# Loading the weights of an attention and gated-MLP kernel in pieces on SyncE's queue, with smaller first tiles and warm products

## The chip, the cores and the metric

The kernel runs on one core of one Trainium2 chip. The metric is the device time of one execution in microseconds (us). Runs come in a fast and a slow state (e9 below: 256.56 to 257.29 us and 263.62 to 265.26 us); only fast runs are compared. "Faster" or "slower" needs 2%.

The engines are named as in the profile: PE is TensorE (PEld its weight load), DVE VectorE, ACT ScalarE, POOL GpSimd, SP SyncE. In the traces TensorE took its products in the order in which the program lists them (compared up to the first `psp` product: 342 products in the changed kernel, 303 in the one before). The weight loads issued on GpSimd convert float32 to float16 on the way (the page of the kernel before counts 256 KB for each of the eight of w_in, whose float32 source is 512 KB); those issued on SyncE bring the float32 bytes (16 of 256 KB for the same matrix), which engines then cast.

## The reference

For each of 8 batches the kernel computes grouped attention (16 query heads, 4 key heads, 384 positions, 64 numbers a head), puts the heads side by side to rows of 1024, and sends them through a gated MLP:

```python
attn = softmax(q @ k.T / 8) @ v            # 16 heads, k and v shared by 4
h = np.maximum(x @ w_in, 0.0)              # w_in 1024 x 1024
u, v = h[..., :512], h[..., 512:]
v_n = (v - mean) / sqrt(var + 1e-6)
v_s = einsum('ts,bsd->btd', w_spatial, v_n) + b_spatial
out = (u * v_s) @ w_out                    # w_out 512 x 1024
```

Inputs and outputs are float32; the products use float16. In this text the "V products" are those with the second half of w_in, the "U group" those with the first half, and "po" those with w_out.

## The kernel before

The program is a written list of steps. Each step goes to the end of the queue of each engine that it uses, so the list fixes the order in which each engine is given its instructions. `lwi` and `lwo` load weights, `lk lq lv` load inputs, `ck cq cv` cast them, `S` is a score product, `E` its exp, `X` the product with v, `V` and `G,..,gu` the V and U products.

```python
FIRST = """                                   # cut to a few steps
lk,0,0,2 lq,0,0,0,1,s cq,0,0,0,1,0,v ck,0,0,s Tk,0,0 cq,0,0,0,1,1,s lk,0,2,4 Tq,0,0,0 ...
lwi,0,1,3 cq,0,0,1,3,0,p lwi,0,1,0 ... lwi,0,1,2 lwi,0,1,1 ... V,0,0,0,4 V,0,0,4,8 ...
... lwi,0,0,2 ... lwi,0,0,0 lwo,0,1 ... lwi,0,0,3 lwi,0,0,1 ... lwo,0,0 ...
"""

    def load_w_in(part, g):                   # one of 8; converts while it loads
        c0, c1 = part * DH, (part + 1) * DH
        nc.gpsimd.dma_start(
            w_in16[32 * g : 32 * (g + 1), :, c0:c1],
            moe_w_in[g * G * D : (g + 1) * G * D, c0:c1].rearrange("(kc r) n -> r kc n", r=32),
        )

    def v_mm(b, st, k0=0, k1=NKT):            # V products: need w_in16[:, kc, 512:1024]
        ...
        for kc in range(k0, k1):
            nc.tensor.matmul(
                held["pv", b, st],
                xT[b][:, kc, st * P : (st + 1) * P],
                w_in16[:, kc, DH:DFF],
                start=(kc == 0), stop=(kc == NKT - 1),
            )
```

Chunk `kc` of `w_in16` needs four groups of 32 rows of w_in that lie 256 rows apart: partition 32g+r holds row 256g+32kc+r.

The softmax here doesn't subtract the row's maximum and nothing guards it: scores larger than these inputs give would overflow.

## Time and profile before

The median of the first three runs is 257.8 us (257.32 to 258.01). The one profile at hand was of a run of 260.65 us, marked slow.

| what | before |
|---|---|
| TensorE busy from 50 to 240 us | 189.4 of 190 us |
| TensorE busy in the first 50 us | 38.4 us |
| wait of the first V products for w_in | 4.21 us |
| first U group | 53.12 us |
| span | 258.8 us |

From the profile page of the kernel before: busy time of TensorE with its share of the span, then busy tenths in 40 slices of 6.5 us.

```profile
PE 242.5 (94%) x2505; PEld 124.1 (48%) x2505; DVE 152.1 (59%) x287; ACT 182.8 (71%) x229; POOL 45.3 (18%) x92
...
PE   2985899899999999999999999999999999999993
...
DMA  7999999894994008995394909293582011300606
```

After the eighth slice TensorE is full. Up to it the DMA row is nearly always at 9: loads set the pace of the start.

The busy time by stretch, kernel before. The first pair is the stretch, the next number its length, then each engine's busy time, the granted clock of TensorE, the mean busy share of the DMA engines (overlapping packets can take it past 1) and GB/s.

```profile
25.00:30.00 5.00, 3.10 (x8) 1.02 (x8) 0.67 (x2) 0.42 (x1) 2.20 (x5) 0.58 1.06 334
0.00:50.00 50.00, 38.39 (x323) 15.87 (x325) 27.65 (x48) 34.65 (x42) 19.56 (x38) 0.93 1.06 219
50.00:240.00 190.00, 189.38 (x2104) 100.25 (x2099) 116.65 (x226) 144.08 (x181) 25.78 (x54) 1.00 0.55 145
```

From the timeline of TensorE, kernel before: start, length, instructions, and in brackets the idle time ahead of them and what ended it.

```profile
26.91 3.57 PE L441 MATMUL pv<-w_in,xt 128*128 128x512 f16 x8 [4.21 <-DMA w_in<-in_moe_w_in_dram]
...
53.12 0.82 PE L616 MATMUL pu<-xt,w_in 64*128 64x384 f16 x8
```

From the chain of waits of the kernel before, in order of time: start, length, what.

```profile
15.68 0.51 POOL w_in L241
16.19 10.58 DMA w_in<-in_moe_w_in_dram
```

One load of 256 KB took 10.58 us, while the DMA engines were full with it and others (busy share 1.06 from 25 to 30 us), and the first V products waited for it.

### The profile page before, as it was taken

Reading aid. Unit: us, or ns where it says so; the run is one execution under the profiler, and the core shown is the slowest. Engines: PE = TensorE matmul, PEld = TensorE weight load, DVE = VectorE, ACT = ScalarE, POOL = GpSimd, SP = SyncE. Lnnn points to the kernel's source line nnn. Section 1 sums busy time; section 2 is a strip of 40 time slices with the busy share of each in tenths; the row PEclk is TensorE's granted clock in tenths of the full one; section 3 lists DMA queues with packets and bytes.
Section 4 is the critical chain, followed back from the end, with each engine's and each line's share of the span. In section 5 each row is a group of like instructions: output and inputs, shape, how many; then the busy total and the mean of one; then the engine's idle time right before and its main releaser. Section 6 shows DMA issues by size and latency. Waiting matters only on the chain.

```text
span 258.8 us, 5938 instructions
## 1 busy us (share of the span) xinstructions
PE 242.5 (94%) x2505; PEld 124.1 (48%) x2505; DVE 152.1 (59%) x287; ACT 182.8 (71%) x229; POOL 45.3 (18%) x92
## 2 busy tenths in 40 slices
PE   2985899899999999999999999999999999999993
...
DMA  7999999894994008995394909293582011300606
GB/s 183 230 265 247 292 196 195 153 286 125 237 262 102 4 3 304 165 345 174 113 205 131 313 8 233 95 323 114 104 214 84 3 55 61 127 6 0 243 0 243
DMA packets 57578, 41.66 MB, mean 161 GB/s; under 512 B 26832, under 2 KB 53840, under 8 KB 57552
## 3 DMA queue, kind: packets, MB, share of 16 engines
...
## 4 chain that ended last, share of the span: by engine, by line
PE 83%; DMA 9%; DVE 4%; ACT 1%; POOL 0%; issue 0%; SPq 0%; ACTq 0%
PE X L398 18%; PE po L643 14%; PE pu L616 12%; PE sc L378 11%; PE pv L603 11%; PE pv L441 5%; DMA w_in<-in_moe_w_in_dram 4%; PE po L548 4%; PE pu L513 4%; PE psp L629 3%; DMA k<-in_k_dram 3%; DMA q<-in_q_dram 2%; DVE v_s L499 1%; DVE v_n L473 1%; PE psp L487 1%; ACT aT L389 1%
## 5 line engine op out<-in xcount | busy, mean ns | idle before, releaser
L389 ACT ACTIVATE aT<-sc 128x1024 f16<-128x1024 f32 x144 | 140.8, 1023 | 35.7 <-PE sc L378 35.3
L643 PE MATMUL po<-w_out,gT 64*128 64x512 f16 x288 | 68.0, 376 | 0.0
L603 PE MATMUL pv<-w_in,xt 64*128 64x512 f16 x272 | 64.9, 376 | 0.0
L378 PE MATMUL sc<-qT,kT 64*128 64x512 f16 x288 | 56.4, 396 | 1.4 <-DVE qT L308 0.5
L427 DVE TENSOR_TENSOR xt<-X,rec 128x512 f16<-128x512 f32 x48 | 31.2, 686 | 13.4 <-ACT rec L415 4.8
L308 DVE COPY osb<-po 128x512 f32<-128x512 f32 x39 | 26.6, 686 | 17.8 <-PE po L643 15.3
L616 PE MATMUL pu<-xt,w_in 64*128 64x384 f16 x384 | 36.7, 323 | 0.0
L398 PE MATMUL X<-aT,v 128*32 128x512 f16 x576 | 35.9, 379 | 0.0
L643 PEld LDWEIGHTS <-gT 64*128 64x128 f16 x288 | 25.4, 94 | 14.5 <-DVE mark_v L697 3.0
L603 PEld LDWEIGHTS <-xt 64*128 64x128 f16 x272 | 24.8, 94 | 12.5 <-issue 3.8
L308 POOL CAST q<-q 128x768 f16<-128x768 f32 (+2 forms) x34 | 24.4, 747 | 35.8 <-DMA q<-in_q_dram 33.2
L525 DVE SCALAR_TENSOR_TENSOR gT<-pu,v_s 128x384 f16<-128x384 f32 x31 | 16.1, 553 | 24.6 <-PE pu L616 20.9
L378 PEld LDWEIGHTS <-kT 64*128 64x128 f16 x288 | 17.1, 94 | 25.2 <-issue 16.9
L616 PEld LDWEIGHTS <-w_in 64*128 64x128 f16 x384 | 20.0, 94 | 13.3 <-issue 0.8
L499 DVE TENSOR_TENSOR v_s<-psp,bias_b 128x384 f32<-128x384 f32 x32 | 20.0, 688 | 5.6 <-PE psp L487 3.4
L398 PEld LDWEIGHTS <-v 128*32 128x32 f16 x576 | 15.9, 96 | 15.5 <-issue 1.6
L398 PE MATMUL X<-aT,ones 128*32 128x512 f16 x288 | 20.6, 392 | 0.5 <-DVE v_s L499 0.2
L409 ACT ACTIVATE rec<-X 128x512 f32<-128x512 f32 x22 | 13.1, 598 | 11.1 <-PE X L398 11.1
L462 DVE BATCH_NORM_STATS2 stats<-v_r 128x6 f32<-128x512 f32 x24 | 16.5, 686 | 5.6 <-ACT v_r L454 2.9
L699 POOL MEMSET mark_p<- 1x1 f32 x20 | 1.8, 88 | 101.4 <-PE psp L629 57.7
L441 PE MATMUL pv<-w_in,xt 128*128 128x512 f16 x56 | 15.3, 419 | 4.2 <-DMA w_in<-in_moe_w_in_dram 4.2
L629 PE MATMUL psp<-wsT,v_n 64*128 64x384 f16 x144 | 15.5, 323 | 0.9 <-DVE v_n L473 0.8
...
## 6 DMA issues: line engine op xcount, KB each, us to landing
...
```

Of the source, the lines that this page charges most:

```text
L308: engine.tensor_copy(dst, src)
L378: mm = nc.tensor.matmul(sc[:, half, :], kT[b][lo:hi, gp, t, :], rhs[lo:hi, :], start=True, stop=True)
L389: nc.scalar.activation(aT[b, qt][:, gp, t], held["sc", b, u], AF.Exp, scale=scale)
L398: nc.tensor.matmul(dst[32 * g : 32 * (g + 1), :], v16[:, g, t, 32 * part : 32 * (part + 1)] if part < 2 else ones32, a[:, g // 2, t, g % 2 ...
L427: nc.vector.tensor_tensor(xt[:, jj, :, qt * P : (qt + 1) * P], held["X", b, qt, jj].rearrange("p (j q) -> p j q", j=G), held["rec", b, qt] ...
L441: nc.tensor.matmul(held["pv", b, st], xT[b][:, kc, st * P : (st + 1) * P], w_in16[:, kc, DH:DFF], start=(kc == 0), stop=(kc == NKT - 1),)
L462: nc.vector.bn_stats(s6, held["v_r", b, st])
L499: nc.vector.tensor_tensor(held["v_s", b][:, m, :].rearrange("p (t s) -> p t s", t=NST), held["psp", b, m][:, 0:S].rearrange("p (t s) -> p ...
L603: yield lambda kc=kc: nc.tensor.matmul(held["pv", b, st], xT[b][rows, kc, st * P : (st + 1) * P], w_in16[rows, kc, DH:DFF], start=(first a ...
L616: yield lambda kc=kc: nc.tensor.matmul(held["pu", b, mu][:, 0:S], w_in16[rows, kc, mu * P : (mu + 1) * P], xT[b][rows, kc, :], start=(firs ...
L629: yield lambda st=st: nc.tensor.matmul(held["psp", b, m][:, 0:S], held["v_n", b, st][rows, m * P : (m + 1) * P], wsT16[rows, st, :], start ...
L643: yield lambda m=m: nc.tensor.matmul(held["po", b, i], held["gT", b][rows, m, tt * P : (tt + 1) * P], w_out16[rows, m, half * 512 : (half ...
```

## The change

The intent is to free GpSimd of its casting loads (8.6 us from issue to landing at the median for those of w_in), to let each V or U product start on a piece of weights instead of a quarter of all rows, and to start the first scores sooner:

1. All weights come as 24 float32 pieces of 256 KB on SyncE, into five staging buffers. GpSimd (16), VectorE (6) and ScalarE (2) cast them.
2. The first k tile comes alone, the first q tile in even and odd heads, each with a score product of half size.
3. 37 warm products of the identity fill TensorE's idle time near the start, in the hope of a higher clock at the scores.

The diff, cut to its core:

```diff
-    def load_w_in(part, g):
-        ...nc.gpsimd.dma_start(w_in16[32 * g : 32 * (g + 1), :, c0:c1], ...)
+    def load_w(part, i):
+        piece = stage.tile([P, 512], FP32, name=f"w32_{part}_{i}", tag="w32", bufs=5)
+        if part < 2:
+            src = moe_w_in.rearrange("(g kc r) n -> kc g r n", g=HKV, kc=NKT)[
+                i, :, :, part * DH : (part + 1) * DH
+            ]
+        else:
+            m, half = i // 2, i % 2
+            src = moe_w_out[m * P : (m + 1) * P, half * 512 : (half + 1) * 512]
+        nc.sync.dma_start(piece, src)
+        loaded["w32", part, i] = piece
+
+    def cast_w(part, i, engine):
+        ...copy(dst, loaded["w32", part, i], engine)
 ...
-    def score_mm(b, u):
+    def score_mm(b, u, j0=0, js=1):           # js=2: every second head, half the columns
 ...
+    def warm(b, n):
+        ...
+        for _ in range(n):
+            nc.tensor.matmul(dst, ident16, ident16, start=True, stop=True)
 ...
 FIRST (a few of its steps)
-lk,0,0,2 lq,0,0,0,1,s cq,0,0,0,1,0,v ck,0,0,s Tk,0,0 ...
+lq,0,0,1,3 lq,0,0,0,1,0,2,s W,0,3 cq,0,0,0,1,1,0,2,p ... lk,0,0,2,0,1 W,0,3 W,0,28 ...
+... lw,0,1,2 lq,0,1,1,3 lw,0,1,1 ... lw,0,1,0 lv,0 ... lw,0,1,3 ... lq,1,0 lk,1 lw,0,1,6 ...
+... lk,2 ... lq,2,1 ... lw,0,2,1 lw,0,2,2 lw,0,0,6 ... cw,0,0,6,p ... cw,0,0,3,s ...
```

`lw,0,1,2` loads piece 2 of the V half, `lw,0,0,6` piece 6 of the U half, `lw,0,2,..` pieces of w_out; `cw` casts a piece on GpSimd (p), VectorE (v) or ScalarE (s). The source of a w_in piece has the shape [4, 32, 512]: four row groups, 32 rows, 512 numbers.

More of the change, by code (lines that the diff above doesn't have):

```diff
@@ L16 @@
 DVE, ACT = mybir.EngineType.DVE, mybir.EngineType.Activation
+SPLIT = 1
 FIRST = """
-lk,0,0,2 lq,0,0,0,1,s cq,0,0,0,1,0,v ck,0,0,s Tk,0,0 cq,0,0,0,1,1,s lk,0,2,4 Tq,0,0,0 lq,0,1,0,1
-lq,0,0,1,3 lq,0,1,1,3 cq,0,1,0,1,1,p tq,0,0,0,v tk,0,0,s S,0 cq,0,1,0,1,0,v ck,0,1,v E,0 S,0
-lwi,0,1,3 cq,0,0,1,3,0,p lwi,0,1,0 cq,0,1,1,3,0,p Tk,0,1 lk,1 lv,0 Tq,0,1,0 tk,0,1,v tq,0,1,0,v S,0
-lq,1,0 cq,0,0,1,3,1,v E,0 E,0 lq,1,1 S,0 Tq,0,0,1 S,0 S,0 Tq,0,0,2 cq,0,1,1,3,1,p tq,0,0,1,v
-Tq,0,1,1 tq,0,1,1,v S,0 ck,1,1,p tq,0,0,2,v E,0 lwi,0,1,2 lwi,0,1,1 ck,1,0,p S,0 E,0 cv,0,p E,0
@@ L25 @@
-X,0,0,2 S,0 lv,1 lws,0 Tq,0,1,2 S,0 S,0 lbi,0 Tkk,1 rv,0,0 E,0 lk,2 S,0 X,0,0,0 X,0,0,1 lq,2,0
-lq,2,1 E,0 cq,1,0,0,1,1,p E,0 E,0 E,0 S,0 cq,1,0,1,3,0,p cq,1,0,1,3,1,p cq,1,0,0,1,0,p tq,0,1,2,v
-tkk,1,v cq,1,1,0,1,0,p S,0 E,0 xm,0,0,1 X,0,1,2 xm,0,0,0 X,0,1,0 X,0,1,1 S,0 S,0 V,0,0,0,4 V,0,0,4,8
-rv,0,1 S,0 S,0 E,0 E,0 E,0 E,0 cq,1,1,0,1,1,s xm,0,1,0 xm,0,1,1 Tqq,1,0 tqq,1,0,0,v V,0,1,0,4
-ru,0,0,v cq,1,1,1,3,0,v tqq,1,0,1,v cv,1,v E,0 E,0 S,0 S,0 E,0 X,0,2,0 X,0,2,2 X,0,2,1 lwi,0,0,2
-cws,0,0 cws,0,2 cq,1,1,1,3,1,p cws,0,1 lwi,0,0,0 lwo,0,1 cq,2,0,0,3,0,p lwi,0,0,3 lwi,0,0,1
@@ L31 @@
-cq,2,0,0,3,1,p cq,2,1,0,3,0,p ck,2,1,p lwo,0,0 ck,2,0,p cq,2,1,0,3,1,p E,0 rl,0,2 S,0 re,0,2 E,0 S,0
-xm,0,2,1 Tqq,1,1 E,0 xm,0,2,0 V,0,1,4,8 Tw,0,0,2 Tw,0,2,3 S,0 S,0 tqq,1,1,0,s ru,0,1,v tw,0,0,2
-V,0,2,0,4 V,0,2,4,8 bs,0,0 bs,0,1 ru,0,2,v tqq,1,1,1,v E,0 tw,0,2,3 bs,0,2 S,0 E,0 E,0 S,0 X,1,0,2
-rl,1,0 X,1,0,0 X,1,0,1 Tqq,1,2 S,0 re,1,0 S,0 xm,1,0,0 xm,1,0,1 V,1,0,0,4 E,0 dq,2,0 dk,2 V,1,0,4,8
-S,0 rs,0 tqq,1,2,0,v nm,0,2 E,0 tqq,1,2,1,v nm,0,0 nm,0,1 ru,1,0,v G,0,gs,0,0,0,1 S,0 G,0,gs,2,0,0,1
@@ L36 @@
-dq,2,1 lq,3,1 lk,3 E,0 mk,0,gs,0,v G,0,gs,0,1,0,1 S,0 lv,2 lq,3,0 mk,0,gs,2,v G,0,gs,2,1,0,1 E,0 E,0
-sa,0,0 sa,0,1 sa,0,2 sa,0,3 S,0 cq,3,1,0,3,1,p cq,3,1,0,3,0,p X,1,1,2 cq,3,0,0,3,0,p cq,3,0,0,3,1,p
-X,1,1,1 X,1,1,0 E,0 rl,1,1 re,1,1 ck,3,0,p xm,1,1,0 xm,1,1,1 G,0,gu,0,0,0 S,0 G,0,gu,0,0,1 E,0 S,0
-mk,0,gu,0,v G,0,gu,2,0,0 S,0 E,0 E,0 G,0,gu,0,1,0 S,0 G,0,gu,2,0,1 S,0 G,0,gu,0,1,1 mk,0,gu,2,v E,0
-E,0 E,0 bs,1,0 G,0,gu,2,1,0 S,0 G,0,gu,2,1,1 S,0 gt,0,0 E,0 X,1,2,0 gt,0,2 gt,0,3 gt,0,1 X,1,2,2
@@ L41 @@
-cv,2,v E,0 S,0 S,0 V,1,1,0,4 rl,1,2 V,1,1,4,8 S,0 G,0,go,0,0,0 G,0,go,0,0,1 mk,0,go,0,v S,0 re,1,2
-E,0 E,0 G,0,go,0,1,0 E,0 G,0,go,0,1,1 S,0 E,0 xm,1,2,0 oc,0,1,v oc,0,0,v E,0 X,2,0,2 X,1,2,1 rl,2,0
-xm,1,2,1 re,2,0 ru,1,1,s X,2,0,0 X,2,0,1 S,0 S,0 xm,2,0,0 G,1,w12,2,0,0 G,1,w12,2,0,1 S,0 S,0
-ck,3,1,s E,0 E,0 mk,1,w12,2,v xm,2,0,1 G,1,w12,2,1,0 bs,1,1 G,1,w12,2,1,1 oc,0,2,v ru,1,2,v oc,0,3,v
-E,0 bs,1,2 E,0 X,2,1,2 rl,2,1 re,2,1 X,2,1,0 dq,3,0 S,0 xm,2,1,0 G,2,w24,0,0,0 E,0 lq,4,0
-G,2,w24,0,0,1 S,0 lv,3 dk,3 lq,4,1 rs,1 st,0,0 mk,2,w24,0,p nm,1,0 dq,3,1 nm,1,1 X,2,1,1 S,0
@@ L47 @@
-G,2,w24,0,1,0 E,0 S,0 xm,2,1,1 E,0 oc,0,4,v G,2,w24,0,1,1 nm,1,2 E,0 G,1,gs,0,0,0,1 S,0 cv,3,p
-mk,1,gs,0,p ru,2,0,s oc,0,5,v S,0 G,1,gs,2,0,0,1 mk,1,gs,2,v E,0 G,1,gs,0,1,0,1 G,1,gs,2,1,0,1 S,0
-E,0 S,0 sa,1,0 sa,1,2 sa,1,1 E,0 E,0 sa,1,3 G,1,gu,0,0,0 G,1,gu,0,0,1 S,0 E,0 mk,1,gu,0,p
-G,1,gu,2,0,0 S,0 G,1,gu,2,0,1 S,0 G,1,gu,0,1,0 S,0 E,0 mk,1,gu,2,p G,1,gu,2,1,0 S,0 G,1,gu,0,1,1 E,0
-gt,1,1 gt,1,0 S,0 G,1,gu,2,1,1 E,0 X,2,2,2 E,0 rl,2,2 E,0 gt,1,3 gt,1,2 X,2,2,1 S,0 G,2,w10,1,0,0
-G,2,w10,1,0,1 S,0 E,0 S,0 re,2,2 E,0 mk,2,w10,1,v xm,2,2,1 bs,2,0 G,2,w10,1,1,0 G,2,w10,1,1,1
@@ L53 @@
-oc,1,0,v oc,1,1,v ru,2,1,v X,2,2,0 xm,2,2,0 bs,2,1 lv,4 st,1,0 lk,4 st,0,1 st,0,2 E,0
+lq,0,0,1,3 lq,0,0,0,1,0,2,s W,0,3 cq,0,0,0,1,1,0,2,p cq,0,0,0,1,0,0,2,v lk,0,0,2,0,1 W,0,3 W,0,28
+lq,0,0,0,1,1,2 lk,0,0,2,1,3 lk,0,2,4 lq,0,1,0,1 ck,0,0,0,1,v lw,0,1,2 lq,0,1,1,3 lw,0,1,1
+cq,0,0,0,1,0,1,2,s ck,0,0,1,3,s cq,0,0,1,3,1,0,1,p lw,0,1,0 lv,0 Tq,0,0,0,0,2 lw,0,1,3
+cq,0,0,0,1,1,1,2,p Tk,0,0,0,1 lq,1,0 lk,1 lw,0,1,6 cq,0,1,0,1,1,0,1,p lw,0,1,5 lw,0,1,4 Tq,0,0,0,1,2
+tk,0,0,0,1,v tq,0,0,0,0,2,v S,0 tq,0,0,0,1,2,v ck,0,1,0,3,v Tk,0,0,1,3 S,0 tk,0,0,1,3,v Tk,0,1,0,3
@@ new lines @@
+lw,0,1,7 S,0 S,0 E,0 E,0 cq,0,0,1,3,0,0,1,s cq,0,1,0,1,0,0,1,v tk,0,1,0,3,v Tq,0,1,0,0,1
+tq,0,1,0,0,1,v Tq,0,0,1,0,1 S,0 E,0 Tq,0,0,2,0,1 S,0 W,0,3 tq,0,0,1,0,1,v tq,0,0,2,0,1,v
+cq,0,1,1,3,0,0,1,v cq,0,1,1,3,1,0,1,v S,0 E,0 E,0 E,0 E,0 S,0 Tq,0,1,1,0,1 S,0 Tq,0,1,2,0,1 lq,1,1
+cv,0,p lws,0 tq,0,1,1,0,1,v cw,0,1,0,v cw,0,1,2,p cw,0,1,1,p cw,0,1,3,p tq,0,1,2,0,1,v lw,0,0,2 S,0
+E,0 cq,1,0,1,3,0,0,1,p cq,1,0,0,1,0,0,1,p cq,1,0,0,1,1,0,1,p ck,1,0,0,3,p lv,1 cw,0,1,5,p cw,0,1,7,p
+cq,1,0,1,3,1,0,1,p ck,1,1,0,3,p X,0,0,2 S,0 lw,0,0,3 X,0,0,1 lw,0,0,4 lw,0,0,0 rv,0,0 lq,2,0
@@ new lines @@
+cq,1,1,0,1,0,0,1,p E,0 E,0 E,0 lw,0,0,7 lw,0,0,5 lw,0,0,1 S,0 S,0 cws,0,0 X,0,0,0 E,0 S,0
+cq,1,1,1,3,0,0,1,p lbi,0 lk,2 E,0 X,0,1,2 E,0 rl,0,1 X,0,1,1 S,0 S,0 lq,2,1 E,0 lw,0,2,1 lw,0,2,2
+lw,0,0,6 E,0 cws,0,1 re,0,1 cw,0,0,2,p cws,0,2 cq,1,1,1,3,1,0,1,p xm,0,0,0 xm,0,0,1 cw,0,0,0,p
+Tk,1,0,0,3 tk,1,0,0,3,v cw,0,1,4,v cw,0,1,6,v V,0,0,0,4 X,0,1,0 cq,2,0,0,3,1,0,1,p S,0 Tq,1,0,0,0,1
+V,0,0,4,8 E,0 S,0 xm,0,1,0 xm,0,1,1 tq,1,0,0,0,1,v cw,0,0,4,p cw,0,0,5,p S,0 E,0 V,0,1,0,4
+Tk,1,1,0,3 E,0 S,0 X,0,2,2 cq,1,1,0,1,1,0,1,v ru,0,0,v E,0 Tq,1,1,0,0,1 V,0,1,4,8 rl,0,2
@@ new lines @@
+tq,1,1,0,0,1,s S,0 ru,0,1,v tk,1,1,0,3,v ck,2,1,0,3,p cq,2,0,0,3,0,0,1,p S,0 X,0,2,0 re,0,2 X,0,2,1
+cw,0,0,7,p cq,2,1,0,3,1,0,1,p E,0 S,0 cq,2,1,0,3,0,0,1,p xm,0,2,0 E,0 cw,0,2,1,p cw,0,0,6,p Tw,0,2,3
+Tq,1,0,1,0,1 E,0 cw,0,0,3,s xm,0,2,1 cv,1,v bs,0,0 V,0,2,0,4 S,0 tq,1,0,1,0,1,v tw,0,2,3 S,0
+Tq,1,1,1,0,1 V,0,2,4,8 tq,1,1,1,0,1,v bs,0,1 ru,0,2,v bs,0,2 E,0 S,0 E,0 X,1,0,2 S,0 E,0
+Tq,1,1,2,0,1 Tw,0,0,2 rl,1,0 tw,0,0,2 X,1,0,0 X,1,0,1 re,1,0 E,0 xm,1,0,0 rs,0 xm,1,0,1 S,0 S,0
+Tq,1,0,2,0,1 E,0 E,0 cw,0,0,1,s V,1,0,0,4 V,1,0,4,8 nm,0,0 S,0 nm,0,2 tq,1,1,2,0,1,v nm,0,1
@@ new lines @@
+tq,1,0,2,0,1,v G,0,gs,0,0,0,1 S,0 ru,1,0,v G,0,gs,2,0,0,1 mk,0,gs,0,v mk,0,gs,2,v ck,2,0,0,3,v
+dq,2,0 G,0,gs,0,1,0,1 E,0 dk,2 lw,0,2,0 lw,0,2,3 dq,2,1 G,0,gs,2,1,0,1 S,0 sa,0,1 sa,0,3 lw,0,2,5
+sa,0,0 sa,0,2 lw,0,2,7 lw,0,2,6 cw,0,2,3,p cw,0,2,5,p lw,0,2,4 cw,0,2,6,p cw,0,2,7,p E,0 E,0 S,0
+X,1,1,2 rl,1,1 re,1,1 X,1,1,1 X,1,1,0 lv,2 S,0 G,0,gu,0,0,0 lk,3 lq,3,1 lq,3,0 G,0,gu,0,0,1 E,0
+xm,1,1,0 cv,2,p xm,1,1,1 S,0 cw,0,2,2,v mk,0,gu,0,v cw,0,2,0,v G,0,gu,2,0,0 S,0 G,0,gu,2,0,1 S,0 E,0
+E,0 mk,0,gu,2,v G,0,gu,0,1,0 S,0 G,0,gu,0,1,1 S,0 G,0,gu,2,1,0 E,0 gt,0,0 gt,0,1 S,0 E,0 E,0 E,0 E,0
@@ new lines @@
+X,1,2,2 G,0,gu,2,1,1 S,0 gt,0,2 gt,0,3 cq,3,1,0,3,1,0,1,p ck,3,0,0,3,p cq,3,0,0,3,0,0,1,p
+ck,3,1,0,3,p cq,3,1,0,3,0,0,1,p cq,3,0,0,3,1,0,1,p S,0 V,1,1,0,4 E,0 rl,1,2 E,0 cw,0,2,4,v V,1,1,4,8
+S,0 E,0 G,0,go,0,0,0 S,0 G,0,go,0,0,1 mk,0,go,0,v ru,1,1,v S,0 G,0,go,0,1,0 G,0,go,0,1,1 oc,0,0,v
+oc,0,1,v S,0 E,0 E,0 re,1,2 X,2,0,2 X,1,2,0 rl,2,0 E,0 re,2,0 X,1,2,1 X,2,0,1 X,2,0,0 xm,1,2,0
+xm,1,2,1 xm,2,0,1 S,0 G,1,w12,2,0,0 G,1,w12,2,0,1 bs,1,0 xm,2,0,0 mk,1,w12,2,v S,0 S,0 E,0 E,0 E,0
+G,1,w12,2,1,0 G,1,w12,2,1,1 bs,1,1 oc,0,2,s ru,1,2,v X,2,1,2 X,2,1,0 X,2,1,1 S,0 S,0 bs,1,2 oc,0,3,v
@@ new lines @@
+rl,2,1 st,0,0 dq,3,0 dk,3 re,2,1 st,0,1 dq,3,1 xm,2,1,0 rs,1 E,0 lv,3 lq,4,0 G,2,w24,0,0,0
+G,2,w24,0,0,1 nm,1,0 mk,2,w24,0,v xm,2,1,1 nm,1,1 nm,1,2 S,0 S,0 G,2,w24,0,1,0 E,0 E,0 oc,0,4,v E,0
+G,2,w24,0,1,1 ru,2,0,s oc,0,5,v S,0 S,0 G,1,gs,0,0,0,1 G,1,gs,2,0,0,1 E,0 E,0 mk,1,gs,0,v
+mk,1,gs,2,v G,1,gs,0,1,0,1 G,1,gs,2,1,0,1 S,0 sa,1,0 sa,1,1 S,0 sa,1,3 sa,1,2 G,1,gu,0,0,0
+G,1,gu,0,0,1 G,1,gu,2,0,0 S,0 E,0 E,0 mk,1,gu,0,v bs,2,0 S,0 G,1,gu,0,1,0 E,0 E,0 G,1,gu,0,1,1 S,0
+G,1,gu,2,0,1 E,0 S,0 gt,1,1 gt,1,0 mk,1,gu,2,v X,2,2,1 X,2,2,2 S,0 G,1,gu,2,1,0 S,0 G,1,gu,2,1,1 E,0
@@ L54 @@
+rl,2,2 X,2,2,0 re,2,2 S,0 E,0 xm,2,2,1 gt,1,3 E,0 gt,1,2 G,2,w10,1,0,0 G,2,w10,1,0,1 mk,2,w10,1,v
+S,0 S,0 G,2,w10,1,1,0 xm,2,2,0 E,0 E,0 G,2,w10,1,1,1 E,0 ru,2,1,s lv,4 lq,4,1 lk,4 oc,1,0,v bs,2,1
+oc,1,1,v st,1,0 cv,3,p st,0,2
 """
 STEADY = """
-X,0,0,2 rl,0,0 re,0,0 X,0,0,0 X,0,0,1 S,0 E,0 xm,0,0,0 xm,0,0,1 ck,1,0,p ck,1,1,p cq,1,0,0,3,0,p
-cq,1,0,0,3,1,p cq,1,1,0,3,0,p cq,1,1,0,3,1,p cv,1,p dk,1 dq,1,0 dq,1,1 G,-1,w12,2,0,0 G,-1,w12,2,0,1
-mk,-1,w12,2,v S,0 E,0 S,0 E,0 G,-1,w12,2,1,0 oc,-2,2,v G,-1,w12,2,1,1 ru,-1,2,v oc,-2,3,v st,-2,1
@@ L60 @@
-bs,-1,2 X,0,1,2 rl,0,1 re,0,1 X,0,1,0 X,0,1,1 rs,-1 S,0 E,0 xm,0,1,0 xm,0,1,1 nm,-1,0 nm,-1,1
-G,0,w24,0,0,0 G,0,w24,0,0,1 mk,0,w24,0,v nm,-1,2 S,0 E,0 S,0 E,0 G,0,w24,0,1,0 oc,-2,4,v
-G,0,w24,0,1,1 ru,0,0,s oc,-2,5,v st,-2,2 bs,0,0 lk,2 lq,2,0 lq,2,1 lv,2 S,0 E,0 G,-1,gs,0,0,0,1
-mk,-1,gs,0,p S,0 E,0 G,-1,gs,2,0,0,1 mk,-1,gs,2,p G,-1,gs,0,1,0,1 sa,-1,0 sa,-1,1 S,0 E,0
-G,-1,gs,2,1,0,1 sa,-1,2 sa,-1,3 X,0,2,2 rl,0,2 re,0,2 X,0,2,0 X,0,2,1 S,0 E,0 xm,0,2,0 xm,0,2,1
-G,-1,gu,0,0,0 G,-1,gu,0,0,1 mk,-1,gu,0,p S,0 E,0 G,-1,gu,2,0,0 G,-1,gu,2,0,1 mk,-1,gu,2,p S,0 E,0
@@ L66 @@
-G,-1,gu,0,1,0 G,-1,gu,0,1,1 gt,-1,0 gt,-1,1 S,0 E,0 G,-1,gu,2,1,0 G,-1,gu,2,1,1 gt,-1,2 gt,-1,3 S,0
-E,0 S,0 E,0 G,0,w10,1,0,0 G,0,w10,1,0,1 mk,0,w10,1,v S,0 E,0 S,0 E,0 G,0,w10,1,1,0 oc,-1,0,v
-G,0,w10,1,1,1 ru,0,1,v oc,-1,1,v st,-1,0 bs,0,1 S,0 E,0
+X,0,0,2 rl,0,0 re,0,0 X,0,0,0 X,0,0,1 S,0 E,0 xm,0,0,0 xm,0,0,1 ck,1,0,0,3,p ck,1,1,0,3,p
+cq,1,0,0,3,0,0,1,p cq,1,0,0,3,1,0,1,p cq,1,1,0,3,0,0,1,p cq,1,1,0,3,1,0,1,p cv,1,p dk,1 dq,1,0
+dq,1,1 G,-1,w12,2,0,0 G,-1,w12,2,0,1 mk,-1,w12,2,v S,0 E,0 S,0 E,0 G,-1,w12,2,1,0 oc,-2,2,v
@@ new lines @@
+G,-1,w12,2,1,1 ru,-1,2,v oc,-2,3,v st,-2,1 bs,-1,2 X,0,1,2 rl,0,1 re,0,1 X,0,1,0 X,0,1,1 rs,-1 S,0
+E,0 xm,0,1,0 xm,0,1,1 nm,-1,0 nm,-1,1 G,0,w24,0,0,0 G,0,w24,0,0,1 mk,0,w24,0,v nm,-1,2 S,0 E,0 S,0
+E,0 G,0,w24,0,1,0 oc,-2,4,v G,0,w24,0,1,1 ru,0,0,s oc,-2,5,v st,-2,2 bs,0,0 lk,2 lq,2,0 lq,2,1 lv,2
+S,0 E,0 G,-1,gs,0,0,0,1 mk,-1,gs,0,p S,0 E,0 G,-1,gs,2,0,0,1 mk,-1,gs,2,p G,-1,gs,0,1,0,1 sa,-1,0
+sa,-1,1 S,0 E,0 G,-1,gs,2,1,0,1 sa,-1,2 sa,-1,3 X,0,2,2 rl,0,2 re,0,2 X,0,2,0 X,0,2,1 S,0 E,0
+xm,0,2,0 xm,0,2,1 G,-1,gu,0,0,0 G,-1,gu,0,0,1 mk,-1,gu,0,p S,0 E,0 G,-1,gu,2,0,0 G,-1,gu,2,0,1
@@ L69 @@
+mk,-1,gu,2,p S,0 E,0 G,-1,gu,0,1,0 G,-1,gu,0,1,1 gt,-1,0 gt,-1,1 S,0 E,0 G,-1,gu,2,1,0 G,-1,gu,2,1,1
+gt,-1,2 gt,-1,3 S,0 E,0 S,0 E,0 G,0,w10,1,0,0 G,0,w10,1,0,1 mk,0,w10,1,v S,0 E,0 S,0 E,0
+G,0,w10,1,1,0 oc,-1,0,v G,0,w10,1,1,1 ru,0,1,v oc,-1,1,v st,-1,0 bs,0,1 S,0 E,0
 """
@@ L204, in load_v, with load_q @@
         loaded["v32", b] = v32
-    def load_q(b, gp, t0=0, t1=NST, queue=None):
+    def load_q(b, gp, t0=0, t1=NST, j0=0, js=1, queue=None):
         if ("q32", b, gp) not in loaded:
@@ L210, in load_q @@
         (queue or nc.sync).dma_start(
-            loaded["q32", b, gp][:, :, t0 * D : t1 * D],
-            q[b, h0 : h0 + 2 * G].rearrange("h (p t) d -> p h (t d)", t=NST)[
+            loaded["q32", b, gp][:, j0::js, t0 * D : t1 * D],
+            q[b, h0 + j0 : h0 + 2 * G : js].rearrange("h (p t) d -> p h (t d)", t=NST)[
                 :, :, t0 * D : t1 * D
@@ L215, in load_q, with cast_k @@
         )
-    def cast_k(b, gp, engine):
+    def cast_k(b, gp, t0, t1, engine):
         if ("k16", b) not in loaded:
@@ L220, in cast_k @@
         k32 = loaded["k32", b].rearrange("p (gp h) (t d) -> p gp t h d", gp=NGP, t=NST)
-        copy(loaded["k16", b][:, gp], k32[:, gp], engine)
+        copy(loaded["k16", b][:, gp, t0:t1], k32[:, gp, t0:t1], engine)
     def cast_v(b, engine):
@@ L226, in cast_v, with cast_q @@
         loaded["v16", b] = v16
-    def cast_q(b, gp, t0, t1, half, engine):
+    def cast_q(b, gp, t0, t1, half, j0, js, engine):
         if ("q16", b, gp) not in loaded:
@@ L232, in cast_q @@
             )
-        dst = loaded["q16", b, gp][:, t0:t1, :, half, :]
-        src = loaded["q32", b, gp][:, half * G : (half + 1) * G, :].rearrange(
+        dst = loaded["q16", b, gp][:, t0:t1, j0::js, half, :]
+        src = loaded["q32", b, gp][:, half * G + j0 : (half + 1) * G : js, :].rearrange(
             "p j (t d) -> p t j d", t=NST
@@ L237, in cast_q @@
         copy(dst, src, engine)
-    def load_w_in(part, g):
-        c0, c1 = part * DH, (part + 1) * DH
-        nc.gpsimd.dma_start(
-            w_in16[32 * g : 32 * (g + 1), :, c0:c1],
-            moe_w_in[g * G * D : (g + 1) * G * D, c0:c1].rearrange("(kc r) n -> r kc n", r=32),
-        )
-    def load_w_out(h):
-        nc.gpsimd.dma_start(
-            w_out16[:, 2 * h : 2 * h + 2, :],
-            moe_w_out[2 * h * P : (2 * h + 2) * P, :].rearrange("(m p) n -> p m n", p=P),
-        )
+    def load_w(part, i):
[10 more added lines that the diff above has]
+    def cast_w(part, i, engine):
+        if part < 2:
+            dst = w_in16[:, i, part * DH : (part + 1) * DH]
+        else:
+            m, half = i // 2, i % 2
+            dst = w_out16[:, m, half * 512 : (half + 1) * 512]
+        copy(dst, loaded["w32", part, i], engine)
     def load_ws():
@@ L308, in copy, with transpose_k @@
             engine.tensor_copy(dst, src)
-    def transpose_k(b, gp):
+    def transpose_k(b, gp, t0, t1):
         k16 = loaded["k16", b]
-        pk = bank([P, NST, P], FP16, f"pk_{b}_{gp}")
-        for t in range(NST):
-            nc.tensor.transpose(pk[:, t, :], k16[:, gp, t, :, :].rearrange("p h d -> p (h d)"), ident16)
-        held["pk", b, gp] = pk
-    def take_k(b, gp, engine):
+        pk = bank([P, t1 - t0, P], FP16, f"pk_{b}_{gp}_{t0}")
+        for t in range(t0, t1):
+            nc.tensor.transpose(
+                pk[:, t - t0, :], k16[:, gp, t, :, :].rearrange("p h d -> p (h d)"), ident16
+            )
+        held["pk", b, gp, t0] = pk
@@ L318, in take_k, with transpose_q @@
+    def take_k(b, gp, t0, t1, engine):
         if b not in kT:
             new_kT(b)
-        copy(kT[b][:, gp], held["pk", b, gp], engine)
-        read(f"pk_{b}_{gp}")
-    def transpose_q(b, gp, qt):
+        copy(kT[b][:, gp, t0:t1], held["pk", b, gp, t0], engine)
+        read(f"pk_{b}_{gp}_{t0}")
+    def transpose_q(b, gp, qt, j0, js):
         q16 = loaded["q16", b, gp]
-        pq = bank([P, G, P], FP16, f"pq_{b}_{gp}_{qt}")
-        for j in range(G):
+        pq = bank([P, G // js, P], FP16, f"pq_{b}_{gp}_{qt}_{j0}")
+        for n, j in enumerate(range(j0, G, js)):
@@ L327, in transpose_q, with take_q @@
             nc.tensor.transpose(
-                pq[:, j, :], q16[:, qt, j, :, :].rearrange("p h d -> p (h d)"), ident16
+                pq[:, n, :], q16[:, qt, j, :, :].rearrange("p h d -> p (h d)"), ident16
             )
-        held["pq", b, gp, qt] = pq
-    def take_q(b, gp, qt, engine):
+        held["pq", b, gp, qt, j0] = pq
+    def take_q(b, gp, qt, j0, js, engine):
         if (b, gp) not in qT:
             new_qT(b, gp)
-        copy(qT[b, gp][:, qt], held["pq", b, gp, qt], engine)
-        read(f"pq_{b}_{gp}_{qt}")
```

63 lines of the change are left out of this document (24 added, 39 removed).

## The prediction

> **What bounds it now.** The table of busy time by stretch shows TensorE busy 189 of the 190 us from 50 to 240 us: bound there, and the change leaves that steady state alone. The first 50 us hold 11.6 us of TensorE idle and a half-speed clock (granted 0.58 from 25 to 30 us). Loads set the pace there: the DMA row stays at 9 tenths until about 48 us. The chain of waits runs through one 10.6 us transfer of w_in to 26.9 us; TensorE waits 4.2 us for it, and the next eight V products take 446 ns each where later ones take about half. First score products: 6.26 us. First U group: 53.2 us; 205.6 us follow.
>
> **What the change does.** GpSimd's casting transfers (q0: 8% of 16 engines' span) become 24 float32 pieces of 256 KB on SyncE, plus 24 casts of 128x512 (about 0.6 us each by the trace's 128x512 casts, 14 us, mostly on GpSimd, busy 18%). Splitting the first tiles and the half-size units may start scores no earlier: a 512 KB q load now stands ahead of the k tile on SyncE. Warm products fill idle time[...]. If the pieces spread over all 16 engines, I estimate 2 to 10 us gained, about 250.5 us.
>
> **Why I expect a loss.** A w_in piece reads [4, 32, 512] (four row groups outermost) into 128 partitions. [...] Each of the 16 pieces then puts 64 KB on each of the same four engines. Packets of 1536 B took 65 ns and of 4608 B 186 ns, so I estimate 85 ns for 2 KB: 2.7 us a piece, 44 us for 16, while q, k, v and w_spatial need their share (estimate 28 us) of those engines in the same queue. w_out pieces are fine.
>
> In SyncE's order, the eighth V piece then lands at about 37 us (before: 26.8) and the last U piece at about 73 us, cast at 74. TensorE runs in order, so V of tile 0 stalls until about 38 us and the first U group until about 74 us instead of 53.2: 21 us late[...]. All of that is on the critical path, since TensorE has no slack afterwards.
>
> **Prediction.** 275 us, range 250 to 289. Faster by over 2%: 0.20; within: 0.07; slower: 0.73.
>
> **What would show it.** Right: w_in issue to landing several us[...]; DMA share well below full from 10 to 70 us though loads are pending; TensorE waiting for a w_in cast (GpSimd or VectorE) at V near 30 us and long at U near 60 to 74 us; steady state unchanged. Wrong: pieces landing evenly in 16 parts, U near 45 us, about 250 us.
>
> **What would make it wrong.** [...]four engines running faster alone than 24 B/ns each; pieces slowed by other traffic or blocked casts (then beyond 289).

The four engines are the author's assumption. The changed kernel's trace and e1 to e3 bear it out afterwards: a piece landed in four parts, and in 2, 8 and 16 with another outermost size.

What the traces show for the rest: the 85 ns for 2 KB lie between 65 ns for 1536 bytes and 186 ns for 4608 bytes (23.6 and 24.8 bytes per ns; medians, kernel before). The record does not say what the 28 us come from; in that trace the packets of the queue of the q, k, v and w_spatial loads take 26.7 us of 16 engines' time if those begun before 40 us are counted, and 30.9 us before 48 us. The V products of 446 ns ran at a granted clock of 0.50; later ones took 238 ns each at a clock of 1.00 (1.90 us for the eight at 39.17 us, kernel before). In the changed kernel a w_out piece landed in 16 parts, 3.5 us after its issue.

## The result, and the profile after

The changed kernel gives a correct result and takes 288.33 us (median of 4 fast runs, 287.85 to 288.73), against 257.9 us (257.32 to 258.63, 4 fast runs). The ratio is 1.118, with a 95% interval of 1.114 to 1.121. A ratio here is always the mean time of one kernel's fast runs over that of the other's of the same rounds, so not quite the ratio of the medians.

From the profile page of the changed kernel, whose slices are 7.2 us:

```profile
PE 251.5 (88%) x2544; PEld 127.5 (44%) x2544; DVE 150.0 (52%) x301; ACT 184.6 (64%) x233; POOL 49.3 (17%) x96
...
PE   6757539970886999999999999999999999999994
...
DMA  8764663457695949829873857496646101110415
```

TensorE now has holes up to the thirteenth slice, and the DMA row mostly stands at 3 to 7 there, where it stood at 9. The steady part is as full as before.

The busy time by stretch of the changed kernel, columns as above:

```profile
10.00:40.00 30.00, 18.14 (x134) 5.73 (x132) 10.42 (x17) 15.11 (x17) 4.92 (x9) 0.73 0.59 160
60.00:70.00 10.00, 2.57 (x29) 1.38 (x29) 0.96 (x4) 0.00 (x0) 2.00 (x3) 0.82 0.73 205
```

From 10 to 40 us the DMA engines are busy 0.59 of the time on average, though weight pieces are pending all that time. From 60 to 70 us TensorE works 2.57 us and ScalarE nothing at all.

The timeline of TensorE in the changed kernel, the entries with the long waits:

```profile
22.96 1.47 PE L397 MATMUL X<-aT,v 128*32 128x512 f16 x12 [4.01 <-POOL v L330]
...
38.05 1.44 PE L440 MATMUL pv<-w_in,xt 128*128 128x512 f16 x3 [5.45 <-DVE w_in L330]
42.02 0.59 PE L440 MATMUL pv<-w_in,xt 128*128 128x512 f16 x1 [2.53 <-POOL w_in L330]
...
71.72 0.61 PE L370 MATMUL sc<-qT,kT 64*128 64x512 f16 x2 [9.15 <-ACT aT L383]
...
77.16 1.14 PE L615 MATMUL pu<-xt,w_in 64*128 64x384 f16 x12
79.99 0.50 PE L615 MATMUL pu<-xt,w_in 64*128 64x384 f16 x4 [1.70 <-POOL w_in L330]
...
92.12 0.61 PE L642 MATMUL po<-w_out,gT 64*128 64x512 f16 x4 [2.33 <-DVE w_out L330]
```

The V products wait for casts of pieces, the U group starts at 77.16 us and lacks its last piece until 79.99 us. The wait of 9.15 us is put down to an exp on ScalarE. The timeline of ScalarE tells what held that exp:

```profile
57.91 1.92 ACT L383 ACTIVATE aT<-sc 128x1024 f16<-128x1024 f32 x2
70.13 0.63 ACT L328 ACTIVATE w_in<-w 128x512 f16<-128x512 f32 x1 [10.30 <-DMA w<-in_moe_w_in_dram]
70.67 2.83 ACT L383 ACTIVATE aT<-sc 128x1024 f16<-128x1024 f32 x3
```

ScalarE had the cast of a weight piece next in its order and waited 10.30 us for that piece to land, with exps standing behind it. So the late loads reach TensorE also through an engine that had other work to do.

The chain of waits of the changed kernel up to the U group:

```profile
59.35 12.20 DMA k<-in_k_dram
...
72.15 0.81 POOL q L330
72.96 0.57 POOL w_in L330
...
73.54 5.73 DMA w<-in_moe_w_in_dram
...
79.32 0.62 POOL w_in L330
```

The last U piece is issued only at 73.54 us. It waits for a staging buffer that a GpSimd cast frees, and that cast stands behind casts of k and q of the third batch; k took 12.20 us to land, against a median of 6.2 us for the k loads of 384 KB in this profile. Waits for such buffers are the longest entry among SyncE's waits in the first 80 us (total, times, longest):

```profile
SPq L263 <- POOL w_in L330: 11.4, 5, 4.4
```

### The profile page after: what moved, and what is told of

It is laid out like the page before. It is cut to its first block, busy times and chain, and to the rows that moved or that the text cites. A ratio compares the mean times of both kernels' runs of the same rounds, so it can differ in the third digit from the quotient of the medians.

```text
span 286.9 us, 6066 instructions
## 1 busy us (share of the span) xinstructions
PE 251.5 (88%) x2544; PEld 127.5 (44%) x2544; DVE 150.0 (52%) x301; ACT 184.6 (64%) x233; POOL 49.3 (17%) x96
## 4 chain that ended last, share of the span: by engine, by line
PE 67%; DMA 19%; SPq 6%; DVE 3%; POOL 1%; ACT 1%; issue 1%; ACTq 0%; DVEq 0%; POOLq 0%
PE X L397 15%; PE po L642 12%; PE pu L615 10%; PE pv L602 10%; PE sc L370 9%; DMA w<-in_moe_w_in_dram 7%; DMA k<-in_k_dram 4%; DMA v<-in_v_dram 4%; PE po L547 3%; PE pu L512 3%; DMA w<-in_moe_w_out_dram 3%; PE psp L628 3%; SPq L276 2%; DMA q<-in_q_dram 2%; SPq L263 2%; DVE v_s L498 2%
## 5 line engine op out<-in xcount | busy, mean ns | idle before, releaser
L383 ACT ACTIVATE aT<-sc 128x1024 f16<-128x1024 f32 (+1 forms) x145 | 141.0, 1017 | 51.6 <-PE sc L370 51.5
L370 PE MATMUL sc<-qT,kT 64*128 64x512 f16 (+1 forms) x290 | 56.4, 398 | 10.5 <-ACT aT L383 10.3
L397 PE MATMUL X<-aT,v 128*32 128x512 f16 x576 | 38.3, 400 | 4.0 <-POOL v L330 4.0
L426 DVE TENSOR_TENSOR xt<-X,rec 128x512 f16<-128x512 f32 x48 | 31.1, 685 | 14.4 <-PE X L397 6.2
L330 DVE COPY osb<-po 128x512 f32<-128x512 f32 x38 | 26.0, 686 | 18.3 <-PE po L642 15.9
L370 PEld LDWEIGHTS <-kT 64*128 64x128 f16 x290 | 17.5, 95 | 39.8 <-issue 31.1
L330 POOL CAST q<-q 128x768 f16<-128x768 f32 (+3 forms) x35 | 24.6, 726 | 19.0 <-DMA q<-in_q_dram 17.9
L615 PEld LDWEIGHTS <-w_in 64*128 64x128 f16 x384 | 19.3, 94 | 15.6 <-POOL w_in L330 2.1
L397 PE MATMUL X<-aT,ones 128*32 128x512 f16 x288 | 22.0, 413 | 0.5 <-DVE v_s L498 0.2
L408 ACT ACTIVATE rec<-X 128x512 f32<-128x512 f32 x23 | 13.7, 597 | 9.7 <-PE X L397 9.5
L628 PE MATMUL psp<-wsT,v_n 64*128 64x384 f16 x144 | 14.9, 322 | 0.0
```

The costliest lines, as they stand in the source:

```text
L330: engine.tensor_copy(dst, src)
L370: nc.tensor.matmul(sc[:, half, 0 : 512 // js], kT[b][lo:hi, gp, t, :], qT[b, gp][lo:hi, qt, j0::js], start=True, stop=True,)
L383: nc.scalar.activation(aT[b, qt][:, gp, t].rearrange("p h (j q) -> p h j q", j=G)[:, :, j0::js], held["sc", b, u, j0][:, :, 0 : 512 // js] ...
L397: nc.tensor.matmul(dst[32 * g : 32 * (g + 1), :], v16[:, g, t, 32 * part : 32 * (part + 1)] if part < 2 else ones32, a[:, g // 2, t, g % 2 ...
L426: nc.vector.tensor_tensor(xt[:, jj, :, qt * P : (qt + 1) * P], held["X", b, qt, jj].rearrange("p (j q) -> p j q", j=G), held["rec", b, qt] ...
L615: yield lambda kc=kc: nc.tensor.matmul(held["pu", b, mu][:, 0:S], w_in16[rows, kc, mu * P : (mu + 1) * P], xT[b][rows, kc, :], start=(firs ...
```

## The experiments

Eleven kernels were run: e1 to e4 in the first call, e5_rows32, e6, e7 and e8 in the second, b0, e5_pairs and e9 in the third. Kernels of one call share their runs of the kernel before: 258.23 us (256.94 to 258.93, 7 fast runs), 258.26 us (256.06 to 259.29, 7 fast) and 258.1 us (256.19 to 259.32, 10 fast and one slow). The calls ran on different chips, so a run is compared with the kernel before of its own call first.

**Theory A:** a w_in piece with four row groups outermost moves on four DMA engines only; the bytes queued on these four are what is late. No trace here names the engine of a packet. The number of engines is read from the parts in which a transfer lands, and from the packets under way at one time: in the changed kernel's first 62 us, 2 KB packets of w_in are under way for 47.1 us, exactly four of them for 27.9 us, fewer for 13.0 and five or six for 6.2. **Rival B:** the casts by other engines, or the order on SyncE's queue, are what is late. **Rival C:** the rest of the change (split tiles, warm products, order) costs or gains something of its own.

### e1_outer16: the same bytes with 16 groups outermost

```diff
-            src = moe_w_in.rearrange("(g kc r) n -> kc g r n", g=HKV, kc=NKT)[
+            src = moe_w_in.rearrange("(a kc b) n -> kc a b n", a=16, kc=NKT)[
```

The piece has the same 128 rows' worth of bytes in the same 2 KB rows, but other rows, so the result is wrong. Only the outermost size changes, and with it which rows are read.

> The changed kernel with one thing altered: each w_in piece reads 128 other rows, as 16 groups of 8 rows (outermost size 16 in place of 4). Same bytes, same 2 KB rows, same queue, order, buffers, casts and waits; the result is wrong on purpose (weight rows permuted). Theory A (the outermost size 4 confines a piece to 4 of 16 engines, and that is the loss): a piece lands in 16 parts, the first U product starts near 45 us, and the time is about 251 us (246 to 257). Theory B (the loss comes from the pieces as such: 24 transfers in SyncE's one queue, five buffers, 24 casts on GpSimd and VectorE): unchanged, 283 to 292 us.

It took 257.77 us (257.64 to 258.7, 4 fast runs), ratio 0.999, interval 0.995 to 1.004. Its busy time by stretch, the issues of its w_in pieces on SyncE (count, then shortest, median and longest issue in ns, then first and last start) and its U group:

```profile
10.00:40.00 30.00, 27.72 (x276) 11.11 (x274) 19.68 (x37) 27.57 (x34) 11.43 (x21) 1.00 1.04 272
```

```profile
L263 SPq DMA_DIRECT2D w<-in_moe_w_in_dram x16: 536/548/2458, 4.0 to 45.7; - x16
```

```profile
47.87 1.14 PE L615 MATMUL pu<-xt,w_in 64*128 64x384 f16 x12
51.34 0.50 PE L615 MATMUL pu<-xt,w_in 64*128 64x384 f16 x4 [2.34 <-POOL w_in L330]
```

The whole loss is gone with one number changed, while casts, order and queue stayed. The DMA share from 10 to 40 us rose from 0.59 to 1.04. Theory A holds and B is not needed for the loss. The gain of some 7 us that was expected beyond it did not come: with pieces that land in 16 parts the kernel is as fast as before, not faster. The last U piece is again issued late (45.69 us in the chain of waits, behind a k load of 5.65 us and GpSimd casts) and costs 2.34 us.

### e2_outer8 and e3_outer2: eight and two groups outermost

The same edit with `a=8` and with `a=2`, both wrong.

> As e1, with 8 groups of 16 rows (outermost size 8). Theory A: 8 engines, 16 packets of some 87 ns each a piece, 22 us for 16 pieces on each of them plus some 28 us of other loads: last U piece near 50 to 54 us, time 253 to 264 us. Theory B: 283 to 292 us.

> As e1, with 2 groups of 64 rows (outermost size 2). Theory A: 2 engines, 64 packets of some 87 ns a piece, 5.6 us a piece and 89 us for 16, plus some 28 us of other loads: last U piece near 120 us, time 315 to 345 us. Theory B: 283 to 292 us.

They took 269.96 us (ratio 1.047, interval 1.041 to 1.053) and 328.01 us (ratio 1.272, interval 1.265 to 1.279), two fast runs each. The last wait of the U group and the issues of w_in pieces, for e2:

```profile
62.56 0.50 PE L615 MATMUL pu<-xt,w_in 64*128 64x384 f16 x4 [2.05 <-POOL w_in L330]
```

```profile
L263 SPq DMA_DIRECT2D w<-in_moe_w_in_dram x16: 598/636/2887, 4.0 to 57.9; - x16
```

And for e3:

```profile
118.98 0.82 PE L615 MATMUL pu<-xt,w_in 64*128 64x384 f16 x4 [3.33 <-POOL w_in L330]
```

```profile
L263 SPq DMA_DIRECT2D w<-in_moe_w_in_dram x16: 544/3149/7347, 4.0 to 110.3; - x16
```

The same line of the changed kernel itself:

```profile
L263 SPq DMA_DIRECT2D w<-in_moe_w_in_dram x16: 532/1456/5910, 3.9 to 73.5; - x16
```

| outermost size | median us | last wait of U ends, us | span after it, us | median issue of a piece, ns |
|---|---|---|---|---|
| 2 | 328.0 | 118.98 | 207.4 | 3149 |
| 4 (the change) | 288.3 | 79.99 | 206.9 | 1456 |
| 8 | 270.0 | 62.56 | 206.1 | 636 |
| 16 | 257.8 | 51.34 | 205.6 | 548 |

The fourth column is the span of the profiled run less the third. It is the same within 2 us, so the outermost size acts almost wholly through the time at which the U group has its weights, and by at most 2 us through what comes later. The smaller the outermost size, the longer the issue of a piece also holds SyncE (548, 636, 1456 and 3149 ns at the median for 16, 8, 4 and 2). The trace's semaphore record of the changed kernel agrees with four engines: a piece gives one entry at once and then four as it lands (one piece at 16.49, 16.80, 16.82 and 17.44 us). The other three runs go the same way, and so answer whether the other rows that they read could be the cause. In e3 a piece gives one entry (8.69 us) and then two (21.43 and 21.67 us); in e2 one (7.92 us) and then eight (15.19 to 15.62 us); in e1 none at once and sixteen as it lands (11.92 to 12.77 us). The number of parts in which a piece lands is the outermost size each time.

### e4_gpsimd: the change with the old weight loads

`load_w` and `cast_w` are taken out, and the loads of the kernel before stand on GpSimd near the places where its casts of weights stood. All else of the change is kept. The result is correct.

```diff
-    def load_w(part, i): ...nc.sync.dma_start(piece, src)...
-    def cast_w(part, i, engine): ...
+    def load_w_in(part, g): ...nc.gpsimd.dma_start(w_in16[32 * g : 32 * (g + 1), :, c0:c1], ...)
```

> The changed kernel with the weights loaded as before (GpSimd's casting transfers, no pieces, no casts by engines), all else of the change kept: the split first tiles, the half-size units, the warm products, the new order of steps. Theory A and theory B both: the loss goes, 250 to 258 us. Theory C (the split, the warm products or the new order cost by themselves): stays above 265 us. Against e1 it tells whether pieces that use all engines beat the casting transfers.

It took 256.9 us (254.98 to 257.75, 4 fast runs), ratio 0.995, interval 0.989 to 1.001. That answers rival C: everything but the weight loads is worth nothing that 2% would notice. Its U group starts at 49.42 us and 206.5 us follow.

### e7_nowarm: e4 without the 37 warm products

```diff
-lq,0,0,1,3 lq,0,0,0,1,0,2,s W,0,3 cq,... lk,0,0,2,0,1 W,0,3 W,0,28 lq,...
+lq,0,0,1,3 lq,0,0,0,1,0,2,s cq,... lk,0,0,2,0,1 lq,...
```

> e4 without the 37 warm products. In e4 score pairs still take 0.60 us until 12 us and 0.39 us from 14 us on, as before the change or 1 to 2 us sooner. If the warm products bring the full clock forward, the time rises by 1 to 2 us over e4; if ScalarE's exponentials and the loads bound that stretch, it stays within 0.7 us of e4.

A later `W,0,3` goes too. Its three fast runs took 256.44, 256.98 and 257.23 us (a fourth was slow), ratio 0.996, interval 0.988 to 1.004. Their median is within 0.1 us of that of e4. It was run on another chip. The timeline of TensorE tells why. First e4, with warm products ahead of the scores, then e7:

```profile
10.80 0.57 PE L320 MATMUL sc<-qT,kT 64*128 64x512 f16 x2
11.63 0.39 PE L320 MATMUL sc<-qT,kT 64*128 64x512 f16 x2
```

```profile
10.93 0.39 PE L320 MATMUL sc<-qT,kT 64*128 64x512 f16 x2
11.59 0.39 PE L320 MATMUL sc<-qT,kT 64*128 64x512 f16 x2
```

A pair of score products takes 0.39 us at full speed, and it reaches that at 10.93 us without warm products and at 11.63 us with them (so the expectation's "0.39 us from 14 us on" misread e4). The granted clock from 7.8 to 11.2 us was 0.50 in e4 and 1.00 in e7: with the warm products, most of them over by 4.9 us, the clock was the lower one there (only the first pair, of half size, was the faster with them: 0.28 us against 0.40 us, at 7.4 us). TensorE waits for exps there in any case (0.46 and 0.52 us before the next pairs in e7), so its speed is not what binds.

### e5_rows32: a correct load that lands in 16 parts, four DMAs to a piece

```diff
-            src = moe_w_in.rearrange("(g kc r) n -> kc g r n", g=HKV, kc=NKT)[...]
+            for g in range(HKV):
+                r0 = g * G * D + 32 * i
+                nc.sync.dma_start(
+                    piece[32 * g : 32 * (g + 1)],
+                    moe_w_in[r0 : r0 + 32, part * DH : (part + 1) * DH],
+                )
```

> The changed kernel, correct, with each w_in piece loaded by four transfers of 32 rows (64 KB each, outermost size 32) in place of one of [4, 32, 512]: 64 transfers in place of 16, all else kept. If the engine count is the whole cause, a piece lands in 16 parts per transfer and the time falls to that of e1 or a few us more for the added issues (48 of about 0.45 us each, some 22 us of SyncE's time in the first 60 us): 256 to 263 us. If SyncE's issue time binds instead, V and U wait for late issues and it stays at 264 us or more.

It took 268.33 us (267.85 to 269.2, 4 fast runs), ratio 1.041, interval 1.035 to 1.046. The U group starts at 61.02 us. Each transfer of 64 KB now lands in 16 parts, by the semaphore record. Two thirds of the loss are recovered. For the rest the trace points to SyncE:

```profile
L259 SPq DMA_DIRECT2D w<-in_moe_w_in_dram x64: 310/419/1982, 3.9 to 54.6; - x64
```

The 64 issues take 27 us at their median of 419 ns (64 times 0.419), SyncE is issuing nearly without a break from 16 to 50 us, and these issues are 23% of the chain of waits from 20 to 70 us. That they are the whole rest is not shown: the test of it, e5_pairs, missed.

### e5_pairs: a correct load with half as many issues

```diff
-        piece = stage.tile([P, 512], FP32, ..., bufs=5)
+        piece = stage.tile([P, 2, 512], FP32, ..., bufs=2)     # two chunks of kc
+            for g in range(HKV):                                # 128 KB each
+                r0 = g * G * D + 64 * pair
+                nc.sync.dma_start(
+                    piece[32 * g : 32 * (g + 1)],
+                    moe_w_in[r0 : r0 + 64, ...].rearrange("(kc r) n -> r kc n", r=32),
+                )
```

> Correct: w_in in pairs of k chunks, 128 rows in four transfers of 32 partitions and 128 KB each[...]; two staging buffers of two chunks. The same bytes on SyncE's queue, with half as many issues as the version of four 64 KB transfers a piece (268.3 us, SyncE at 0.42 us an issue). If the engines are the cause and SyncE's issues were what that version lost on: 32 + 4 issues instead of 72, so half of its 10 us come back, 258 to 264 us, U group at 50 to 56 us. If the spread over 16 engines were not what counts, it stays near 288. The smaller number of staging buffers may cost a microsecond or two.

It took 271.36 us (269.5 to 272.79, 4 fast runs), ratio 1.051, interval 1.046 to 1.055: the expected 258 to 264 us was missed, and the U group starts at 59.50 us, not at 50 to 56. The chain of waits shows what took the place of the issues:

```profile
44.87 0.52 ACT w_in L336
45.45 0.31 SPq L262
...
47.88 6.06 DMA k<-in_k_dram
...
55.14 4.03 PE X L405 x29
```

SyncE issued nothing from 38.60 to 45.45 us: it waited for one of the two staging buffers, which a ScalarE cast freed at 45.4 us. The k load behind it in SyncE's order came late by that. With a third buffer of this size the program does not build, so whether 32 issues with deeper staging would reach 258 us stays open.

### e8_act: other loads moved to ScalarE's queue

The changed kernel, with v of the first batch and k and half of q of the second issued on ScalarE instead of SyncE. It asks whether SyncE's long issues hold up loads that could go on other engines, or whether the bytes on the four engines bind.

```diff
-lv,0 ... lq,1,0 lk,1
+lv,0,s ... lq,1,0,0,3,0,1,s lk,1,0,4,0,3,s
```

> The changed kernel (4-engine pieces kept), with v of batch 0 and q and k of batch 1 issued by ScalarE's queue, so that they don't stand behind the pieces in SyncE's. Theory A1 (bytes on the four engines): v lands earlier than 21.9 us and the first X with v moves up by several us, but the last U piece and the first U group stay near 79 us, the time within 3 us of 288. Theory A2 (the pieces hold SyncE's issue, up to 5.9 us each, and so the loads behind them; the four engines run dry meanwhile): the U group comes 6 us or more earlier, 275 to 282 us.

It took 290.62 us (two fast runs, ratio 1.127), no better than the change. The U group starts at 79.89 us and has its last piece at 83.17 us (77.16 and 79.99 us in the change). The cast of v does come earlier (15.5 against 22.1 us), but the first product with it comes later (28.26 against 22.96 us). So taking these issues off SyncE did not help here. The test is not a clean one: ScalarE was itself held, and its scores with it:

```profile
20.80 0.61 PE L327 MATMUL sc<-qT,kT 64*128 64x512 f16 x2 [10.14 <-ACT aT L340]
```

### b0_before: the kernel before, profiled once more

> The kernel before once more, for a profile in the fast state: the one profile of it so far came from a run of 260.65 us, span 258.8, while its other runs took 257.3 to 258.6. If the rest of the change is worth nothing, this profile (span near 256) should show the first U group where the versions without the four-engine loads have it, at 50 to 51 us, with about 206 us after it. If it shows U at 53 again and a span of 256, then the stretch after U is 203 us here, and the changed kernel's U group at 50 has gained 3 us which it gives back later.

It took 257.18 us, span 255.4. This is a single run, so its state is called unknown, but its time lies among the fast runs of the same call. The timeline of TensorE:

```profile
25.13 3.00 PE L441 MATMUL pv<-w_in,xt 128*128 128x512 f16 x8 [2.93 <-DMA w_in<-in_moe_w_in_dram]
...
48.89 0.82 PE L616 MATMUL pu<-xt,w_in 64*128 64x384 f16 x8
```

In this run, the only ordinary one with a profile, the U group starts at 48.89 us, not at 53.12 us, and 206.5 us follow. That is why e1 (51.34 us) and e4 (49.42 us) gain nothing: the start that they seemed to shorten was never that long. The profile that the prediction was read from had a start 4.2 us too late.

### e6_early and e9_best: attempts to beat both

e6 is e4 with the second half of the V weights issued before GpSimd's casts of q and v. e9 is e6 without warm products, with k of the third batch cast on GpSimd and transposed by DMA ahead of q.

```diff
 e6: -... cv,0,p lwi,0,1,2 lwi,0,1,1 ...
     +lwi,0,1,3 cq,0,1,0,1,1,0,1,p lwi,0,1,0 lwi,0,1,2 lwi,0,1,1 ...
 e9: -ck,2,0,0,3,v dq,2,0 ... dk,2 dq,2,1
     +ck,2,1,0,3,p ck,2,0,0,3,p ... dk,2 dq,2,0 ... dq,2,1
```

> e4 (GpSimd's casting loads, the rest of the change) with the second half of V's weights issued ahead of v's cast on GpSimd, so some 3 us sooner. In e4 TensorE waits 2.4 us for them at 21.7 us and the clock falls after it. If that wait still bounds the start, 2 to 4 us less than e4: 252 to 255 us. If the transfers only delay v and the second batch's q and k by the same bytes, within 1 us of e4.

In e4 that wait, of 2.38 us, ends at 24.07 us; the granted clock is 0.99 from 20 to 25 us and 0.67 from 25 to 30 us.

> A try at beating both: the changed kernel with its weights by GpSimd's casting transfers as before, the V half issued early, no warm products, and k of the third batch cast on GpSimd and transposed by DMA ahead of q, so that the scores of that batch no longer wait 1.5 us for its kT. The V wait of 2.4 us and the kT wait are gone: U at 46 to 47 us, span 251 to 253, so 253 to 255 us, a ratio of 0.98 to 0.99. Rival: the start does not bound the end by that much (some later wait takes it up), 257 to 258 us.

e6 took 255.69, 258.27 and 258.83 us in its fast runs (ratio 0.999, interval 0.990 to 1.007); e9 took 256.56, 257.02 and 257.29 us (ratio 0.995, interval 0.991 to 0.998). Each also had slow runs of 262 to 265 us, one of four for e6 and three of six for e9. The wait of the V products for w_in is gone in both, and a later wait takes its place. From the waits of TensorE (total, times, longest), first e6, then e9:

```profile
PE sc L320 <- DMA kT<-k: 1.5, 1, 1.5
```

```profile
PE sc L320 <- DMA qT<-q: 2.3, 1, 2.3
```

e6 has its U group at 46.52 us and then waits for the transposed k of the third batch. e9 removed that wait, has its U group at 47.35 us, and then waits 2.27 us at 53.68 us for the transposed q instead, whose transpose now stands behind that of k. From its U group to the end e9 takes 208.2 us, 1 to 2 us more than b0 and e4 (206.5 us each) and e6 (207.4 us). No version that clearly beats both kernels was found.

## Why the prediction was right or wrong

The direction and the mechanism were right; the loss was 13 us larger than the 275 us said, though within the range.

- **Four engines.** Right as far as the runs show it, though no run had shown it when the prediction was written. Changing only the outermost size gave 328, 288, 270 and 258 us for 2, 4, 8 and 16, and a piece landed in 2, 4, 8 and 16 parts; in the changed kernel four 2 KB packets at a time was the usual number (27.9 of 47.1 us). That they are the same four for each piece shows in the other loads on that queue: of the 16 parts of v, issued at 10.22 us, twelve landed from 15.32 to 16.14 us and four from 20.98 to 22.03 us, just behind the four of the piece ahead of it (19.67 to 21.11 us) and before those of the piece behind it (24.27 to 25.21 us).
- **The waits.** Right in kind: the V products waited for casts by VectorE and GpSimd (5.45 and 2.53 us), the DMA share from 10 to 40 us was 0.59, a piece gave one entry at once and four as it landed, and the steady part was unchanged. The last of the V waits ended at 42.02 us, not at about 38. Not foreseen was the 4.01 us wait for v, the 10.30 us that ScalarE stood at a weight cast, and the 2.33 us wait for w_out.
- **"The first U group until about 74 us instead of 53.2: 21 us late".** This is the step that failed in size, at both ends. The start in an ordinary run is 48.89 us, as b0 showed; the 53.2 us came from a profile of a slow run. The end is 79.99 us. The true delay is 31.1 us (79.99 less 48.89), which is nearly the whole difference of the two spans (286.9 less 255.4 is 31.5 us). The anchor gives 4.3 us of the miss and the U group 6 us.
- **Why 80 and not 74 us.** The sum held the DMA engines alone and took the four as always busy. Two things speak against it. Packets of 2 KB took 87 ns at the median but 100 ns on average before 62 us, against the 85 ns assumed; over the 512 packets that each of the four engines gets from 16 pieces, 15 ns are 8 us. And the last piece was issued only at 73.54 us, when a cast had freed its staging buffer (the chain of waits after). The two overlap, and no run separates them.
- **What the traces say of these two.** With four engines, packets of one engine overlap at times (five or six of w_in under way for 6.2 us), so a longer packet need not be lost time: in e3 from 40 to 50 us, when almost nothing but w_in moved, 238 packets of 2 KB moved in 10 us. That is 48.7 bytes per ns, or 24.4 for each of two engines, which is the rate that the prediction assumed (2 KB in 85 ns, 24.1). An estimate from the packets of the changed kernel's trace (those of 2 KB on four engines, the others evenly on sixteen) has each of the four busy for only 0.7 of the time from 25 to 30, 40 to 45 and 55 to 60 us, and fully in the other stretches of 5 us between 10 and 60. They ran partly dry, which speaks for the late issues; it is an estimate and not a test.
- **The stated figure.** 258 us plus 21 us, less 1 us for warm products and order, is 278 us. The 275 us given is 3 us less, perhaps a lean towards the branch of 16 engines; the prediction does not say. No gain from warm products came to be subtracted. With the 10 us above that is 14 us, against a miss of 13.3 us; the run b0 was 0.7 us below the median.
- **The other branch.** "If the pieces spread over all 16 engines, I estimate 2 to 10 us gained, about 250.5 us" was wrong: e1 took 257.77 us. The gain was measured from the late start of the slow profile, and the best case for warm products (3 to 4 us) is nothing in e7, which without them took 256.98 us against 256.9 us in e4.
